# One score loop for both halves of K, a loop for the down projection, and start-up code moved to the end of three engines' programs

## The chip, the cores and the metric

The kernel runs on one core of one Trainium2 chip. A core has engines that each follow a program of their own and meet through semaphores: TensorE (PE in the profile, with PEld for its weight loads), VectorE (DVE), ScalarE (ACT), GpSimd (POOL) and SyncE (SP), which here only issues DMA transfers. Sixteen DMA engines move data between the chip's memory and the core's on-chip memory. The metric is the device time of one execution in microseconds; lower is better. Three runs of the kernel before took 2518.41, 2518.26 and 2518.09 us, so its median is 2518.26 us.

## What is computed

One token passes a block of attention with a long cache and a small feed-forward block, and a gate mixes the two results. All data is bf16.

```python
g = sigmoid((x * gate_w).sum(-1))
q = (x @ wq)                                   # 32 heads of 128
scores = q . k_cache * 128 ** -0.5             # 65536 keys a head
o = softmax(scores) . v_cache                  # 65536 values a head
a = o @ wo                                     # 4096 -> 512
b = (silu(x @ w_gate) * (x @ w_up)) @ w_down   # 512 -> 1792 -> 512
out = g * a + (1 - g) * b
```

The K cache and the V cache are 512 MiB each, and every byte of them is used once, so nearly all of the work is the reading of 1 GiB.

## The kernel before

**Tiling.** The 65536 rows of K of one head are cut into two halves, u = 0 and 1, called A and B. A half is one transfer of 8 MiB into the tile `ring`: each of the 128 partitions takes 256 rows of 128 numbers. V is cut in the same way. The regions of `ring` for the two K halves overlap by half of a region, and those of the two V halves by 48 of 64 KB, so a load may start only when a part of the half before it has been used up.

**Order of the loads.** SP holds one queue. For head r it waits until 24 of the 32 transposes of that head are done and issues the A half of the next head's K (lines 168 and 169), waits for `va1` and issues the B half of V, waits until 8 transposes of the next head are done and issues the B half of its K (lines 177 and 178), then waits for `vbd` and issues the A half of V (lines 179 and 180). Line 145 is the helper that issues. The first head's loads, and those of the weights, are issued in pieces; the last V half is loaded in six pieces (`PARTS`), each with a semaphore of its own, behind 11 of the 14 chunks of `w_down`. The last three chunks of `w_down` come at the very end.

**Scores.** A half of K is 16 chunks of 16 rows. For each chunk DVE transposes 128x1024 words from `ring` to one of four buffers `kt` (helper `turn`, line 314), once PE has freed that buffer (`qkd`). PE then runs four matmuls of 512 columns into the one PSUM bank `psS` (helper `scores`, line 401). Their weights are windows of 128 columns of `zq`, a tile of zeros that has q in four of its columns; where the window lies decides into which row of `psS` the scores of the chunk fall. All addresses are constants: 64 matmuls for the A half and 64 for the B half stand in the program one after another. The first matmul of a head clears the bank, the last one closes it.

**Softmax and values.** After the last chunk of the B half DVE takes the row maximum of `psS` (line 338), POOL the maximum over partitions (line 216), ACT the exponentials (line 251), DVE transposes them to `pb` (line 340). PE multiplies V by them: in `flow` (line 417) four rows of V a matmul into `psW`, and for the last rows of the B half in `values` (line 408) one row a matmul into `psO`. Between the two, DVE copies `psW` (line 327, for the last head line 355) and eight small fp32 matmuls fold it into `psO` (line 452).

**PE's program.** It is a set of blocks joined by branches. After a start-up part (lines 363 to 396: a ramp, x, the gate, q for all heads) the blocks run so for each head: `pe_ka` (scores of the A half), `pe_vb` (B half of V of the head before), `pe_kb` (scores of the B half, then the A half of V). Before the last head's `pe_kb` stands `pe_wo`, where the output projection of 31 heads is done by pairs of matmuls (`both`, line 512 and, through `whole`, line 428), four pairs in an iteration of a loop. After the last head's A half of V stands `pe_mlp`: gate and up projection (line 488), then 11 chunks of the down projection written out one after another (through `whole`, line 428), whose sum ACT copies (line 266) and PE adds into the output banks (lines 423 and 424). Then come `pe_vb` for the last head and `pe_end` with the last three chunks of `w_down`, the last head's part of the output projection and the output itself.

**DVE's and POOL's programs** begin with their start-up parts (lines 281 to 308, lines 201 to 213). DVE then loops over the heads; POOL's reductions for the 32 heads stand one after another.

Of the kernel before, what the change touches and what calls it, by code (L numbers as in the profile page):

```python
# [5 lines left out]
P = 128  # L6
# [7 lines left out]
FETCH = 256  # L14
# [12 lines left out]
def bass_gated_mix__mha_block_cached__swiglu_ffn__decode_kernel(  # L27
# [27 lines left out]
    with ExitStack() as ctx:  # L55
# [6 lines left out]
        def sem(name):  # L62
# [47 lines left out]
                 "ktd qkd va1 vbd s_mx s_ar s_nb s_exp s_pb s_L s_li s_otn s_o s_om s_y s_br s_fl s_flc s_id4 s_qr s_qc s_wod s_o31 s_y0 s_y1 s_fin s_out s_hot")  # L110
# [88 lines left out]
        @block.gpsimd  # L199
        def _(pool):  # L200
            nc.gpsimd.memset(xTz[:], 0.0).then_inc(sm["s_qd"], 1)
            nc.gpsimd.memset(qd[:], 0.0).then_inc(sm["s_qd"], 1)
            for m, n in enumerate(MARKS[1:]):
                nc.gpsimd.memset(hbuf[:, m], 0.0).then_inc(sm[n], 16 * L)
            nc.gpsimd.memset(hot[:], 0.0).then_inc(sm["s_hot"], 1)
            pool.wait_ge(sm["s_id"], 1)
            pool.wait_ge(sm["s_hot"], 1)
            nc.gpsimd.tensor_copy(hot[:, 31:128:32], ident[:, P - 4:P])
            for je in range(4):
                off = 64 * (je // 2) + je % 2  # L210
                last = nc.gpsimd.tensor_copy(sel[:, je, :].rearrange("p (g d) -> p g d", g=4),
                                             ident[:, off:off + 63:2].unsqueeze(1).to_broadcast([P, 4, 32]))
            last.then_inc(sm["s_sel"], 1)
            for h in range(H):
                pool.wait_ge(sm["s_mx"], h + 1)
                nc.gpsimd.partition_all_reduce(amx, mxs, P, RMAX).then_inc(sm["s_ar"], 1)  # L216
                pool.wait_ge(sm["s_exp"], h + 2)
                nc.gpsimd.partition_all_reduce(Lt, rsum, P, RADD).then_inc(sm["s_L"], 1)  # L218
# [54 lines left out]
        def _(dve):  # L273
            chain = [0]

            def link(ins):
# [4 lines left out]
            nc.vector.memset(psW[:], 0.0).then_inc(sm["s_fl"], 1)  # L281
            nc.vector.memset(ones1[:], 1.0).then_inc(sm["s_ones"], 1)
            link(nc.vector.memset(onesr[:], 1.0))
            nc.vector.tensor_tensor_scan(ramp[:], onesr[:], onesr[:], 0.0, ALU.mult, ALU.add).then_inc(sm["s_ramp"], 1)
            link(nc.vector.memset(zq[:], 0.0))
            link(nc.vector.memset(lt[:], 0.0))
            nc.vector.memset(guT[:, 0:1], 0.0).then_inc(sm["s_exp"], 1)
            nc.vector.memset(o31[:], 0.0).then_inc(sm["s_otn"], 1)
            nc.vector.memset(st[:], 1.0).then_inc(sm["s_L"], 1)
            nc.vector.memset(psO[:, 0:1], 0.0).then_inc(sm["vbd"], 1)  # L290
            nc.vector.memset(om[:], 0.0).then_inc(sm["qkd"], NB)
            dve.wait_ge(sm["s_rampT"], 1)
            nc.vector.tensor_tensor(ident[:], ramp[:], psQ[:, 0, 0:1].to_broadcast([P, P]),
                                    ALU.is_equal).then_inc(sm["s_id"], 1)
            dve.wait_ge(sm["s_id"], 1)
            nc.vector.reduce_sum(id4[:], ident[:].rearrange("p (g e) -> p e g", g=4)[:, 0:4, :],
                                 AX_X).then_inc(sm["s_id4"], 1)
            dve.wait_ge(sm["s_x"], 32)
            nc.vector.tensor_tensor_reduce(out=xg[0:1, :], in0=xrow[0:1, :], in1=gwrow[0:1, :],
                                           scale=1.0, scalar=0.0, op0=ALU.mult, op1=ALU.add,  # L300
                                           accum_out=sc[0:1, 0:1]).then_inc(sm["s_z"], 1)
            dve.wait_ge(sm["s_xT"], 1)
            dve.wait_ge(sm["s_qd"], 2)
            nc.vector.tensor_copy(xTb, psM[:, 0:Dc]).then_inc(sm["s_xTb"], 1)
            dve.wait_ge(sm["s_e1"], 1)
            link(nc.vector.tensor_scalar_add(sc[:, 2:3], sc[:, 1:2], 1.0))
            link(nc.vector.reciprocal(sc[:, 3:4], sc[:, 2:3]))
            link(nc.vector.tensor_scalar(sc[:, 4:5], sc[:, 3:4], -1.0, 1.0, ALU.mult, ALU.add))
# [7 lines left out]
            with nc.Fori(0, H, engines=[ET.DVE]) as i:  # L316
# [20 lines left out]
                dve.wait_ge(sm["qkd"], i * PER + (PER + NB))  # L337
                nc.vector.reduce_max(mxs, psS[:], AX_X).then_inc(sm["s_mx"], 1)  # L338
                dve.wait_ge(sm["s_exp"], i + 2)
                nc.vector.transpose(pb[:], pa[:]).then_inc(sm["s_pb"], 1)  # L340

            dve.wait_ge(sm["s_otn"], H + 1)
# [19 lines left out]
        def _(pe):  # L362
# [75 lines left out]
            with nc.body("pe_ka", valid_engines=only):  # L438
# [3 lines left out]
                for n, c in enumerate(A_ORDER):  # L442
                    scores(n, c, i, n == 0, False)
# [120 lines left out]
```

## Time and profile before

| | us |
|---|---|
| median of 3 runs | 2518.26 |
| the profiled execution, its own time | 2518.01 |
| its span, first to last instruction | 2516.6 |
| PE busy | 1511.9 |
| DVE busy | 1249.7 |
| DMA queue of SP, share of 16 engines' span | 99.9% |
| mean rate of the DMA | 432 GB/s |
| granted TensorE clock, mean | 0.781 |

A row of the timeline has a start, a duration, the engine, the line of the kernel, the operation with out<-in, a count, and in brackets the idle time before it with what ended it. A row of a window lists the window, its length, and the busy time and count of each engine; at its end stand the granted TensorE clock (1.00 is full speed), the mean busy share of the 16 DMA engines and the rate. In the list of a line's instructions, PEldq is the sequencer that issues PE's instructions, and the durations are the shortest, the median and the longest.

### The profile page before, as it was taken

The page shows a single profiled execution, that of the slowest core. Times are in us where ns is not written, and L with a number is a line of the kernel's source. Part 1 is how long each engine was busy: PE and PEld are TensorE (multiplying, and loading weights), DVE is VectorE, ACT ScalarE, POOL GpSimd, SP SyncE. Part 2 cuts the span into 40 slices and gives each one's busy share as a digit, 9 for nine tenths or more (in the row PEclk, how much of TensorE's full clock was granted, in tenths as well). Part 3 has the DMA queues.
Part 4 walks back from the last instruction along what each step waited for, and adds up shares of the span by engine and source line. Part 5 has one row for each costly group of instructions (what it writes and reads, how often), then busy time and mean ns, then how long its engine had stood idle before and what let it go on. Part 6 is the DMA issues. An engine that isn't in the chain of part 4 may idle for free.

```text
span 2516.6 us, 25250 instructions
## 1 busy us (share of the span) xinstructions
PE 1511.9 (60%) x10158; PEld 573.9 (23%) x10158; DVE 1249.7 (50%) x1213; ACT 43.0 (2%) x142; POOL 25.9 (1%) x81
## 2 busy tenths in 40 slices
PE   4565655745656556566565575565655655656568
PEld 1222222212222222222222121222212222212222
DVE  5454553644545536445455364464553644545534
ACT  0000000000000000000000000000000000000000
POOL 0000000000000000000000000000000000000000
PEclk8877877878778778778787787877877778778788
DMA  9999999999999999999999999999999999999999
GB/s 419 434 433 433 434 433 434 433 434 434 434 433 434 434 433 435 433 432 433 433 433 433 433 433 433 433 433 433 433 434 433 433 433 434 433 433 433 433 432 394
DMA packets 20748, 1087.73 MB, mean 432 GB/s; under 512 B 2307, under 2 KB 2694, under 8 KB 2950
## 3 DMA queue, kind: packets, MB, share of 16 engines
q1 hardware_dynamic: 20736, 1087.64, 99.9%
q8 instruction: 4, 0.07, 0.0%
q14 instruction: 2, 0.02, 0.0%
q10 hardware_dynamic: 6, 0.00, 0.0%
HBM read 1087.64 MB, written 0.00 MB: 432 GB/s over the span
## 4 chain that ended last, share of the span: by engine, by line
DMA 75%; DVE 15%; issue 7%; PE 2%; DVEq 1%; SPq 0%; ACT 0%; POOL 0%
DMA ring<-in_A_k_cache_dram 74%; DVE kt L314 15%; PE psS L401 2%; DMA ring<-in_A_v_cache_dram 1%; DVEq L311 0%; SPq L145 0%; PE psW L417 0%; DVE st L325 0%; PE psY L423 0%; ACT pa L251 0%; DVE pb L340 0%; DVE st L338 0%; DVEq L324 0%; DVE fin L359 0%; SPq L136 0%
## 5 line engine op out<-in xcount | busy, mean ns | idle before, releaser
L401 PE MATMUL psS<-kt,zq 128*128 128x512 bf16 x4096 | 1132.6, 425 | 854.6 <-DVE kt L314 835.3
L314 DVE STREAM_TRANSPOSE kt<-ring 128x1024 uint32<-128x1024 uint32 x1024 | 1163.1, 1206 | 939.7 <-DMA ring<-in_A_k_cache_dram 939.7
L401 PEld LDWEIGHTS psS<-kt,zq 128*128 128x128 bf16 x4096 | 385.1, 104 | 1588.3 <-DVE kt L314 1129.7
L417 PE MATMUL psW<-ring,pb 128*4 128x512 bf16 x3584 | 256.2, 448 | 102.7 <-DVE pb L340 102.4
L417 PEld LDWEIGHTS psW<-ring,pb 128*4 128x4 bf16 x3584 | 94.8, 98 | 262.6 <-issue 187.8
L327 DVE COPY brow<-psW 128x512 f32<-128x512 f32 x32 | 22.1, 691 | 120.5 <-PE psW L417 120.5
L408 PEld LDWEIGHTS psO<-pb,ring 128*128 128x128 bf16 x2048 | 57.0, 98 | 0.5 <-DMA ring<-in_A_v_cache_dram 0.2
L408 PE MATMUL psO<-pb,ring 128*128 128x1 bf16 x2048 | 56.6, 163 | 0.2
L330 DVE TENSOR_SCALAR lt<-psO,st,sc 128x4 f32 x32 | 9.4, 294 | 89.1 <-PE psO L408 89.1
L452 PE MATMUL psO<-id,brow 128*128 128x1 f32 x256 | 33.8, 253 | 25.5 <-DVE brow L327 24.7
L340 DVE STREAM_TRANSPOSE pb<-pa 128x512 bf16<-128x512 bf16 x32 | 22.8, 711 | 48.7 <-ACT pa L251 48.7
L249 ACT ACTIVATE st<-st 128x1 f32<-128x1 f32 x32 | 6.5, 203 | 2358.5 <-POOL st L216 2358.5
L338 DVE TENSOR_REDUCE st<-psS 128x1 f32<-128x512 f32 x32 | 22.1, 692 | 37.4 <-PE psS L401 37.4
L452 PEld LDWEIGHTS psO<-id,brow 128*128 128x128 f32 x256 | 31.0, 191 | 41.7 <-DVE brow L327 40.4
L216 POOL PARTITION_ALL_REDUCE st<-st x32 | 11.2, 351 | 2420.2 <-DVE st L338 2420.2
L251 ACT ACTIVATE pa<-psS,st 128x512 bf16<-128x512 f32 x32 | 22.0, 687 | 1.0
L428 PE MATMUL psF<-ring,om 128*1 (+1 forms) x32 | 12.7, 396 | 2.9 <-DMA ring<-in_A_wo_dram 2.9
L512 PE MATMUL psY<-ring,hot 128*128 (+1 forms) x32 | 13.1, 411 | 0.0
L218 POOL PARTITION_ALL_REDUCE st<-st x32 | 12.3, 383 | 36.4 <-ACT pa L251 36.4
L256 ACT COPY zq<-qd 128x16 bf16 x31 | 7.7, 248 | 0.0
L251 ACT ACTIVATION_READ_ACCUMULATOR pa<-psS,st 128x1 f32 x32 | 6.2, 193 | 0.0
L428 PE MATMUL psF<-ring,kt 128*1 128x512 bf16 x11 | 4.2, 564 | 3.0 <-DVE kt L353 3.0
(87 smaller groups left out, 52.8 us busy)
## 6 DMA issues: line engine op xcount, KB each, us to landing
ring<-in_A_k_cache_dram SPq DMA_DIRECT2D x4, 4096.0 KB, 27.4
ring<-in_A_v_cache_dram SPq DMA_DIRECT2D x3, 2048.0 KB, 17.6
ring<-in_A_wq_dram SPq DMA_DIRECT2D x1, 4096.0 KB, 12.4
ring<-in_A_wo_dram SPq DMA_DIRECT2D x2, 2048.0 KB, 10.6
ring<-in_B_w_gate_dram SPq DMA_DIRECT2D x1, 1792.0 KB, 21.4
ring<-in_B_w_up_dram SPq DMA_DIRECT2D x1, 1792.0 KB, 25.4
ring<-in_B_w_down_dram SPq DMA_DIRECT2D x1, 1408.0 KB, 13.1
ring<-in_A_v_cache_dram SPq DMA_DIRECT2D x1, 1280.0 KB, 20.4
```

The lines of the kernel that those rows point to most:

```text
L218: nc.gpsimd.partition_all_reduce(Lt, rsum, P, RADD).then_inc(sm["s_L"], 1)
L251: nc.scalar.activation(pa[:], psS[:], ACT.Exp, bias=nbias, scale=SCALE, accum_out=rsum).then_inc(sm["s_exp"], 1)
L314: nc.vector.transpose(o, src).then_inc(sm["ktd"], 1)
L327: nc.vector.tensor_copy(brow[:], psW[:]).then_inc(sm["s_flc"], 1)
L338: nc.vector.reduce_max(mxs, psS[:], AX_X).then_inc(sm["s_mx"], 1)
L340: nc.vector.transpose(pb[:], pa[:]).then_inc(sm["s_pb"], 1)
L401: last = nc.tensor.matmul(psS[:], zw[je][c], ktb[n % NB][:, je // 2, :, je % 2], start=first and je == 0, stop=stop and je == 3)
L408: last = nc.tensor.matmul(psO[:, 0:1], at(base + r * 256, Dh), pb[:, col:col + 1], start=first and n == 0, stop=stop and n == len(rows) - 1)
L417: last = nc.tensor.matmul(psW[g:g + 4, :], pb[:, col:col + 97:32], at(base + r * 256, 4 * Dh), start=first and n < 4, stop=stop and n >= l ...
L428: return nc.tensor.matmul(psF[0:1, :], lhs, rhs, start=first, stop=stop)
L452: nc.tensor.matmul(psO[:, 0:1], brow[:, e * Dh:(e + 1) * Dh], id4[:, e:e + 1], start=e == 0, stop=False)
L512: return nc.tensor.matmul(psY[:], hot[:, bass.ds(31 - j, P)], w, start=first, stop=stop)
```

## The change

Four things are changed.

- **One loop for the scores.** A new block `pe_scores` holds four chunks and is run four times for each half. The register `top` (31 for A, 15 for B) and the loop's counter give the window of `zq`, so each of the 16 weight loads of an iteration has an address from a register. `turns` counts the chunks for the wait on `ktd`. The branch at its end goes on by `top`. Since no matmul of the loop can be the first or the last by a constant, a matmul of a row of zeros by 512 zeros clears `psS` ahead of the A half (`clear`) and another one closes it behind the B half (`seal`), and DVE's maximum waits for that last one (`s_ss`) instead of for the count of chunks. The chunks fall into other rows of `psS`; `place` takes that into account for the columns of `pb`. The row of zeros is a row of `xg` that DVE clears at the start.
- **A loop for the down chunks.** Ten of the 11 matmuls in `pe_mlp` become a loop with one matmul an iteration; the eleventh follows it.
- **The output projection's loop** takes two pairs in an iteration and 15 iterations, instead of four pairs and seven.
- **The order of the programs.** On PE, DVE and POOL the program begins with a branch to the start-up part, which now stands behind the code of the heads; from there a branch leads back to the heads. On PE the start-up part stands just ahead of `pe_mlp`, `pe_wo` and `pe_end`. DVE's loop over the heads is written with a register and a branch. The alignment to 256 bytes on PE goes.

```diff
+        zero = xg[32:33, :].bitcast(BF16)
-        zw = [[zq[:, je, 31 - c:31 - c + P] for c in range(2 * NCH)] for je in range(4)]
...
         @block.gpsimd
...
+            nc.br("pool_begin", engines=only)
+            with nc.body("pool_heads", valid_engines=only):
+                for h in range(H):
...
+                nc.br("pool_end", engines=only)
+            with nc.body("pool_begin", valid_engines=only):
+                nc.gpsimd.memset(xTz[:], 0.0).then_inc(sm["s_qd"], 1)
...
+                nc.br("pool_heads", engines=only)
...
         @block.vector
...
+            nc.br("dve_begin", engines=only)
...
-                dve.wait_ge(sm["qkd"], i * PER + (PER + NB))
+                dve.wait_ge(sm["s_ss"], i + 1)
                 nc.vector.reduce_max(mxs, psS[:], AX_X).then_inc(sm["s_mx"], 1)
...
+                nc.vector.memset(xg[32:33, :], 0.0)
...
         @block.tensor
...
+            nc.regs_mov(turns, 0)
+            nc.br("pe_begin", engines=only)
...
+            def clear(out):
+                return nc.tensor.matmul(out, zero[:, 0:P], zero[:, P:P + 512], start=True, stop=False)
+            def seal(out):
+                return nc.tensor.matmul(out, zero[:, 0:P], zero[:, P:P + 512], start=False, stop=True)
+            def add(out, lhs, rhs):
+                return nc.tensor.matmul(out, lhs, rhs, start=False, stop=False)
+            def place(r, u):
+                return (r % CH) * 32 + NCH * u + (r // CH + (4 if u else 12)) % NCH
...
             with nc.body("pe_ka", valid_engines=only):
                 i = nc.snap(head, min_val=0, max_val=L)
                 pe.wait_ge(sm["s_zq"], i + 1)
                 pe.wait_ge(sm["s_exp"], i + 1)
-                for n, c in enumerate(A_ORDER):
-                    scores(n, c, i, n == 0, False)
+                clear(psS[:])
+                nc.regs_mov(top, 31)
+                nc.br("pe_scores", engines=only)
+
+            with nc.body("pe_scores", valid_engines=only):
+                with nc.Fori(4, 4 + NCH, NB, engines=only) as j:
+                    t = nc.snap(turns, min_val=0, max_val=PER * H - NB)
+                    z = (nc.snap(top, min_val=15, max_val=31) - j % NCH).with_bounds(min_val=NB - 1, max_val=31)
+                    for n in range(NB):
+                        pe.wait_ge(sm["ktd"], t + (n + 1))
+                        for je in range(4):
+                            last = add(psS[:], zq[:, je, bass.ds(z - n, P)], ktb[n][:, je // 2, :, je % 2])
+                        last.then_inc(sm["qkd"], 1)
+                    nc.regs_alu(turns, turns, NB, op=ALU.add)
+                nc.br_lt(top, 31, on_true="pe_va", on_false="pe_kad", engines=only)
...
             with nc.body("pe_kb", valid_engines=only):
+                nc.regs_mov(top, 15)
+                nc.br("pe_scores", engines=only)
+
+            with nc.body("pe_va", valid_engines=only):
+                seal(psS[:]).then_inc(sm["s_ss"], 1)
                 i = nc.snap(head, min_val=0, max_val=L)
-                for n, c in enumerate(B_ORDER):
-                    scores(NCH + n, NCH + c, i, False, n == NCH - 1)
                 pe.wait_ge(sm["s_pb"], i + 1)
...
-                for j in range(WD_CUT):
-                    last = whole(guT[:, 32 * j:32 * j + 1], wd_ap[:, j, :], stop=(j == WD_CUT - 1))
-                last.then_inc(sm["s_y"], 1)
+                with nc.Fori(0, WD_CUT - 1, engines=only) as j:
+                    whole(guT[:, bass.ds(j * 32, 1)], wd_ap[:, bass.ds(j, 1), :].rearrange("p c n -> p (c n)"))
+                j = WD_CUT - 1
+                whole(guT[:, 32 * j:32 * j + 1], wd_ap[:, j, :], stop=True).then_inc(sm["s_y"], 1)
...
                 both(0, first=True)
-                with nc.Fori(1, 29, 4, engines=only) as j:
-                    for n in range(4):
-                        both(j + n)
-                both(29)
-                both(30)
+                with nc.Fori(1, 31, 2, engines=only) as j:
+                    both(j)
+                    both(j + 1)
                 both(31, stop=True).then_inc(sm["s_wod"], 1)
```

More of the change, by code (lines that the diff above doesn't have):

```diff
@@ L200, in _ @@
         def _(pool):
[L201 to L218, printed above, removed]
+            only = [ET.Pool]
@@ L279, in link @@
                 dve.wait_ge(sm["s_dch"], chain[0])
[L281 to L308, printed above, removed]
+            only = [ET.DVE]
+            turn_h = nc.alloc_registers("dve_head", engines=only)
+            nc.regs_mov(turn_h, 0)
+            nc.br("dve_begin", engines=only)
             def turn(byte, c, n, i):
@@ L405, in values @@
-            def values(base, u, rows, first, stop):
-                for n, r in enumerate(rows):
-                    col = (r % CH) * 32 + NCH * u + r // CH
-                    last = nc.tensor.matmul(psO[:, 0:1], at(base + r * 256, Dh), pb[:, col:col + 1],
-                                            start=first and n == 0, stop=stop and n == len(rows) - 1)
-                return last
+            only = [ET.PE]
+            head = nc.alloc_registers("pe_head", engines=only)
+            left = nc.alloc_registers("pe_left", engines=only)
```

167 lines of the change are left out of this document (111 added, 56 removed).

## Prediction

> **What bounds the kernel now.** First the page, for the span and the DMA queues, and the list of DMA issues, whose last column is the median time from issue to landing.
>
> ```profile
> span 2516.6 us, 25250 instructions
> DMA packets 20748, 1087.73 MB, mean 432 GB/s; under 512 B 2307, under 2 KB 2694, under 8 KB 2950
> q1 hardware_dynamic: 20736, 1087.64, 99.9%
> q8 instruction: 4, 0.07, 0.0%
> ring<-in_A_v_cache_dram SPq DMA_DIRECT2D x63, 32.4
> ring<-in_A_k_cache_dram SPq DMA_DIRECT2D x62, 29.3
> ```
>
> SP's queue keeps all 16 DMA engines busy for 99.9% of the span: the kernel runs at the rate of its transfers. The second thing to see is the slack. A half of K or V is 8.39 MB, at 432 GB/s 19.4 us of transfer, but from issue to landing a K half takes 29.3 us and a V half 32.4 us. So a K half stands 9.9 us in the queue behind other transfers, a V half 13.0 us. Whatever makes PE or DVE release a region later by less than that leaves no gap.
>
> Then a head from the middle, in the timeline:
>
> ```profile
> 1194.74 2.77 PE L417 MATMUL psW<-ring,pb 128*4 128x512 bf16 x48
> 1199.22 1.77 PE L408 MATMUL psO<-pb,ring 128*128 128x1 bf16 x64
> 1214.16 18.14 DVE L314 STREAM_TRANSPOSE kt<-ring 128x1024 uint32<-128x1024 uint32 x16 [12.73 <-DMA ring<-in_A_k_cache_dram]
> 1215.47 17.97 PE L401 MATMUL psS<-kt,zq 128*128 128x512 bf16 x64 [14.48 <-DVE kt L314]
> 1223.48 0.33 SPq L145 DMA_DIRECT2D ring<-in_A_k_cache_dram  x1
> 1233.48 0.69 DVE L338 TENSOR_REDUCE st<-psS 128x1 f32<-128x512 f32 x1 [1.17 <-PE psS L401]
> ```
>
> DVE waits 12.73 us for the landing, then sets the pace of the scores: 18.14 us for 16 chunks, 1.13 us each, and PE follows. A K issue (1223.48) comes 9.3 us into the stage, after the eighth transpose.
>
> Last the tail, where no later load hides anything:
>
> ```profile
> 2462.49 18.14 DVE L314 STREAM_TRANSPOSE kt<-ring 128x1024 uint32<-128x1024 uint32 x16 [22.63 <-DMA ring<-in_A_k_cache_dram]
> 2464.41 17.35 PE L401 MATMUL psS<-kt,zq 128*128 128x512 bf16 x64
> 2484.96 6.41 PE L417 MATMUL psW<-ring,pb 128*4 128x512 bf16 x64 [3.20 <-DVE pb L340]
> 2500.82 4.22 PE L428 MATMUL psF<-ring,kt 128*1 128x512 bf16 x11 [2.95 <-DVE kt L353]
> 2506.23 1.90 PE L417 MATMUL psW<-ring,pb 128*4 128x512 bf16 x32
> 2508.44 1.04 PE L417 MATMUL psW<-ring,pb 128*4 128x512 bf16 x16 [0.31 <-DMA ring<-in_A_v_cache_dram]
> 2510.28 1.13 PE L452 MATMUL psO<-id,brow 128*128 128x1 f32 x8 [0.80 <-DVE brow L355]
> 2511.54 2.29 PE L408 MATMUL psO<-pb,ring 128*128 128x1 bf16 x64
> 2514.46 0.08 PEld L423 LDWEIGHTS psY<-ring,kt 128*1 128x1 bf16 x1 [0.23 <-DMA ring<-in_B_w_down_dram]
> ```
>
> From the last landing of K (2462.49) on there runs a chain of compute: transposes, softmax, V, the MLP, the down chunks, the last V rows. It meets the last transfers almost in step: PE waited for a piece of V only 0.31 us at 2508.44, and its 64 value matmuls took 2.29 us with the waits for three landings in them, against 1.77 us without. So the tail has two limits half a microsecond apart, and what the change adds to the chain shows at the end.
>
> **The change, part by part.** All is reckoned against the profiled execution, 2518.01 us (1.4 more than its span); the median, 2518.26, lies 0.25 above it.
>
> Price of a loop on PE: the sequencer's instructions of the loop for `wo`, between 2445.0 and 2447.3, and the pace of that loop's matmuls.
>
> ```profile
> L515 PEldq COMPARE_BRANCH  x2: 218/218/219, 2445.0 to 2446.9; - x2
> L515 PEldq FUSED_REGOPS  x2: 83/83/83, 2445.2 to 2447.2; - x2
> L515 PEldq ALU_OP  x1: 36/36/36, 2446.8 to 2446.8; - x1
> L428 PEldq FUSED_REGOPS  x3: 80/80/80, 2445.6 to 2446.4; - x3
> L512 PEldq MOVE  x4: 29/29/29, 2445.4 to 2446.6; - x4
> L512 PEldq FUSED_REGOPS  x4: 51/51/51, 2445.5 to 2446.7; - x4
> 2446.24 0.38 PE L428 MATMUL psF<-ring,om 128*1 x1
> 2446.87 0.38 PE L428 MATMUL psF<-ring,om 128*1 x1
> ```
>
> Branch to branch is 1.9 us (2445.0 to 2446.9). In it lie 14 such instructions, 0.90 us by their durations (218 + 83 + 36 + 3x80 + 4x29 + 4x51), and the issue of eight matmuls; so each costs 0.07 us beside its duration. PE itself needs 0.63 us a pair (2446.24 to 2446.87), 2.5 us an iteration: the sequencer ran ahead there.
>
> *Score loop.* A chunk needs four addresses (0.051 + 0.07 each), a value to wait for (0.036 + 0.07) and a quarter of the loop's edge (branch 0.29, counter 0.11, chunk count 0.11, window 0.24: 0.19): 0.78 us of issue, below DVE's 1.13. So DVE still sets the pace, at no cost. Bounds: nothing, or 1.2 us a chunk if each address takes a move as well (0.10 more), 0.8 us a stage; that is far under the 9.9, and 0.8 in the tail. For a K load to come too late, the first eight transposes would have to lose 9.9 us, that is, a chunk would have to take 2.4 us.
>
> *`clear` and `seal`.* `clear` runs while PE waits 14.48 us for the first chunk: nothing. `seal` is one more matmul between the last chunk and the maximum; four of them make DVE wait 1.17 us, so 0.29. In every head but the last it lies under the 13.0 us of the next V load; in the tail it counts, 0.3. Bounds 0 and 0.6, if the two branches ahead of it (0.29 each) are not covered by the last chunk's matmuls.
>
> *`wo` loop.* Two pairs an iteration need half of the pairs' issue and a whole edge, 2x0.37 + 0.40 = 1.1 us, against PE's 1.26: nothing. If it did fall behind, K's last scores would start later; PE has 0.2 us a chunk to catch up there (17.35 us from 2464.41 on, though it started 1.9 us after DVE).
>
> *Down loop and clock in the tail.*
>
> ```profile
> 2501.60 0.13 PEld L428 LDWEIGHTS psF<-ring,kt 128*1 128x1 bf16 x1 [0.30 <-issue]
> 2502.02 0.13 PEld L428 LDWEIGHTS psF<-ring,kt 128*1 128x1 bf16 x1 [0.30 <-issue]
> 2500.88:2504.30 3.42, 3.42 (x9) 1.04 (x10) 0.00 (x0) 0.00 (x0) 0.00 (x0) 0.50 1.04 441
> 2504.30:2507.70 3.40, 2.73 (x36) 0.86 (x37) 0.00 (x0) 0.57 (x1) 0.00 (x0) 1.00 0.97 412
> ```
>
> An iteration is FUSED_REGOPS, ALU_OP and the branch: 0.083 + 0.036 + 0.218 + 3x0.07 = 0.55 us for a single matmul. Before, the 11 matmuls took 4.22 us and stood ready when `guT` came. Now a move and an address come first (0.1 + 0.15), then ten iterations, 5.5, then the eleventh, 0.5: 6.2, that is 2.0 us more. Bounds: 0.43 us an iteration, the pace of the matmuls before (2501.60, 2502.02), gives +0.7; 0.7, with a second address instruction, +3.5.
>
> The nine down matmuls ran at clock 0.50 with PE wholly busy, and the clock rose to 1.00 for the V rows. With the loop PE streams 0.43 of each 0.55 us, 78%, so the rise may come late. The 48 matmuls of `flow` cost 2.77 us fast (1194.74) and 4.8 slow (6.41 us for 64 at 2484.96). I take the middle, 3.8.
>
> [...]
>
> *Jumps at the start and DVE's extra memset.*
>
> ```profile
> 0.92 0.48 DVE L281 MEMSET psW<- 128x512 f32 x1 [0.92 <-PEq L549]
> 7.86 0.68 DVE L299 CUSTOM_DVE_ANT_0 xg<-xrow,gwrow 1x512 f32<-1x512 bf16 x1 [4.44 <-DMA gwrow<-in_gate_w_dram]
> 24.13 1.25 DVE L314 STREAM_TRANSPOSE kt<-ring 128x1024 uint32<-128x1024 uint32 x1 [14.17 <-DMA ring<-in_A_k_cache_dram]
> 33.72 0.43 SPq L145 DMA_DIRECT2D ring<-in_A_v_cache_dram  x1
> ```
>
> DVE waits 4.44 us for x and then 14.17 us for K. A jump that has to load code, or the memset (at most the 0.48 us of `psW`'s, 128 rows of the same length), costs nothing below 4.4 us, and below 14 us nothing at the end; then it would move the first issue after a transpose, which like the one at 33.72 must come while the first loads still run. POOL's part only prepares tiles for the first head's q, which waits for the same landing.
>
> *Code loads.*
>
> ```profile
> q8 instruction: 1, 0.02, 1.6%
> 2512.00:2513.00 1.00, 0.95 (x36) 0.87 (x34) 0.00 (x0) 0.00 (x0) 0.00 (x0) 0.50 0.72 249
> 2513.00:2514.00 1.00, 0.94 (x25) 0.69 (x22) 0.13 (x1) 0.00 (x0) 0.00 (x0) 0.50 0.28 98
> ```
>
> The first row is of the 4 us from 20 to 24: a packet of code took 1.6% of 16 engines' 4 us, so 1.0 us of one engine. In the last microsecond only 28% of the engines, four or five, still move data: they look like those that carried the four packets. A shorter program has fewer such packets, but a landing waits for the latest engine; only when none is left in the stream does everything land earlier, by about 1 us. I count nothing; bounds 0 and -1.0.
>
> *Sum.* The chain reaches `flow` 0.3 + 2.0 = 2.3 us later: 2508.5. It no longer waits for V; 3.8 us bring it to 2512.3 (before: 2509.5). Copy and fold, 0.80 + 1.13, values in 1.77: 2516.0, where before they ended at 2513.83. That is 2.2; the waits for the last chunks of `w_down` (0.23 for the last) go, so 2.0. **2518.0 + 2.0 = 2520.0 us**, +0.08%.
>
> **The rivals.**
>
> *The chain gets no longer, or the code leaves the stream.* For it: the two limits lie half a microsecond apart, and with a fast `flow` the sum is only +1.0; -1.0 for the code then ends near 2518. With the lower price of the loop as well 2517. Against it: one late engine is enough to hold every landing.
>
> *The loop starves the queue: slower.* Place: K's issue after the eighth transpose. If a chunk takes over 2.4 us, each microsecond beyond the 9.9 opens a gap twice a head, 64 us in all: at 2.6 us a chunk, 1.9 us too much, 2518 + 64x1.9 = 2640. Against it: 0.78, and 1.2 at the most.
>
> *Code is fetched anew at each long jump: slower.* PE's rounds now jump between `pe_scores` and blocks before and behind it. Three packets a head are 93 in 31 heads, 1.0 us of one engine each, 5.8 us spread over 16; PE's own wait stays under the 9.9. 2520.0 + 5.8 = 2525.8. Against it: a head's matmuls before, a thirty-second of all, run over the same code 32 times, yet the span has four such packets in all. [...]
>
> **How the numbers follow.** Forecast (tail longer by 1 to 4.5 us) 0.60; chain hidden or code gone, 2516.8 to 2519, 0.30; starved 0.03; fetched anew 0.04; something that makes it faster by over 0.2%, 0.02; the rest 0.01. 0.2% is 5.0 us, about what a measurement can tell here from no change: below 2513.2 or above 2523.3. The low end of the range is the rival's 2517, the high end the upper price of the loop, +1.5, and a slow `flow`, +1.0, on 2520.0, with half a microsecond for the seal and the addresses: 2523.0. Same takes 0.90, slower 0.08, faster 0.02: the transfers alone, 1087.64 MB in 99.9% of the span, leave nothing to win that size.
>
> **What would show it.** L314 keeps 18.1 us for 16 chunks, q1 99.9%, K 29 us to landing. The down matmuls stand 0.55 us apart, `flow` of the last head starts near 2508.5 and waits for no landing. PE's code packets are fewer than four. The prediction is wrong if the share of q1 falls, if L314 slows, or if the values at the end still wait for V.

## The result, and the profile after

| | before | after |
|---|---|---|
| median of the runs, us | 2518.28 (2517.84 to 2519.28, 22 runs) | 2521.84 (2520.58 to 2523.20, 22 runs) |
| profiled execution, us | 2518.01 | 2521.66 |
| span, us | 2516.6 | 2520.2 |

The ratio of after to before is 1.0014, with an interval of 1.0008 to 1.002: 3.6 us slower, inside the bound of 0.2% below which the prediction counts two times as the same.

First the DMA view of the changed kernel: queues with packets, MB and share of 16 engines, then issues with the median microseconds to landing.

```profile
q1 hardware_dynamic: 20736, 1087.64, 99.8%
q8 instruction: 2, 0.03, 0.0%
...
ring<-in_A_k_cache_dram SPq DMA_DIRECT2D x62, 29.2
```

The stream is what it was: 99.8% against 99.9%, 29.2 us to landing against 29.3. At most 0.3 us is lost in the 31 heads ahead of the tail (the last landing of K below). Code packets (q8) are two instead of four.

The timeline of the changed kernel, a head from the middle and then the tail (start, duration, engine, line, operation, count, and in brackets the idle time before it with what ended it; line 407 are the scores, 434 the down chunks, 416 `flow`, 465 the fold of `psW` into `psO`, 423 the values):

```profile
1214.54 18.14 DVE L299 STREAM_TRANSPOSE kt<-ring 128x1024 uint32<-128x1024 uint32 x16 [12.66 <-DMA ring<-in_A_k_cache_dram]
1216.05 13.34 PE L407 MATMUL psS<-kt,zq 128*128 128x512 bf16 x48 [14.62 <-DVE kt L299]
1223.85 0.33 SPq L144 DMA_DIRECT2D ring<-in_A_k_cache_dram  x1
...
2462.80 18.14 DVE L299 STREAM_TRANSPOSE kt<-ring 128x1024 uint32<-128x1024 uint32 x16 [22.32 <-DMA ring<-in_A_k_cache_dram]
2482.51 0.69 DVE L324 TENSOR_REDUCE st<-psS 128x1 f32<-128x512 f32 x1 [1.57 <-PE psS L404]
2485.67 5.32 PE L416 MATMUL psW<-ring,pb 128*4 128x512 bf16 x64 [3.20 <-DVE pb L326]
2500.79 6.76 PE L434 MATMUL psF<-ring,kt 128*1 x11 [3.30 <-DVE kt L377]
...
2509.16 4.98 PE L416 MATMUL psW<-ring,pb 128*4 128x512 bf16 x48
...
2514.94 1.05 PE L465 MATMUL psO<-id,brow 128*128 128x1 f32 x8 [0.80 <-DVE brow L379]
2515.86 1.77 PE L423 MATMUL psO<-pb,ring 128*128 128x1 bf16 x64
```

DVE transposes 16 chunks in 18.14 us as before and only the first of them waits; K's issue (1223.85) still comes 9.3 us after the first transpose. In the tail the last K half lands 0.3 us later than before (2462.80 against 2462.49), and the down chunks begin at the same moment (2500.79 against 2500.82). Then the chain falls back: 6.76 us for the 11 down chunks (4.22), and 4.98 us for the 48 matmuls of `flow`, which before took 1.90 for 32 and 1.04 for 16. No row of `flow` or of the values waits for a landing any more. The kernel now ends on its chain of compute.

How slow the clock was there, in windows of 3.41 us of the changed kernel (window, length, busy time and count of PE, PEld, DVE, ACT and POOL, granted clock, share of the DMA engines, GB/s):

```profile
2500.04:2503.45 3.41, 2.44 (x5) 0.40 (x5) 0.36 (x1) 0.00 (x0) 0.00 (x0) 0.50 1.03 437
2503.45:2506.86 3.41, 3.14 (x6) 0.48 (x6) 0.00 (x0) 0.00 (x0) 0.00 (x0) 0.50 0.97 414
2506.86:2510.27 3.41, 2.75 (x18) 0.48 (x20) 0.00 (x0) 0.57 (x1) 0.00 (x0) 0.50 0.96 402
2510.27:2513.68 3.41, 3.41 (x36) 1.13 (x32) 0.00 (x0) 0.00 (x0) 0.00 (x0) 0.50 0.75 273
2513.68:2517.09 3.41, 2.61 (x66) 2.15 (x59) 0.69 (x1) 0.00 (x0) 0.00 (x0) 1.00 0.02 6
```

Four such windows, all at 0.50, and full clock only when `flow` is almost done. Only the second lies wholly under the loop: in the first PE waits until 2500.79, the third holds the pause for ACT's copy, and the fourth is `flow` alone, after which the clock rises. The busy column must not be read as streaming here: 3.14 of 3.41 us in the second window is the sum of six modelled durations of 0.58 us or so, while a matmul at half clock keeps PE for 0.43 us (their distance in the tail before) and the next one comes after 0.64. So PE streams 67% of the loop.

### The profile page after: what moved, and what is told of

Read it like the earlier page. It is cut to its first block, busy times and chain, and to the rows that moved or that the text cites. A ratio compares the mean times of both kernels' runs of the same rounds, so it can differ in the third digit from the quotient of the medians.

```text
span 2520.2 us, 30251 instructions
## 1 busy us (share of the span) xinstructions
PE 1533.4 (61%) x10222; PEld 621.1 (25%) x10222; DVE 1251.9 (50%) x1214; ACT 43.0 (2%) x142; POOL 26.4 (1%) x81
## 3 DMA queue, kind: packets, MB, share of 16 engines
q1 hardware_dynamic: 20736, 1087.64, 99.8%
## 4 chain that ended last, share of the span: by engine, by line
DMA 73%; DVE 14%; issue 7%; PE 5%; DVEq 0%; SPq 0%; ACT 0%; POOL 0%
DMA ring<-in_A_k_cache_dram 72%; DVE kt L299 14%; PE psS L407 3%; PE psF L434 1%; DVEq L296 0%; PE psY L569 0%; DMA ring<-in_A_wo_dram 0%; PE psW L416 0%; SPq L144 0%; PE psY L544 0%; DVE st L311 0%; DVE kt L372 0%; PE psY L429 0%; PE psO L423 0%; PE psO L465 0%
## 5 line engine op out<-in xcount | busy, mean ns | idle before, releaser
L299 DVE STREAM_TRANSPOSE kt<-ring 128x1024 uint32<-128x1024 uint32 x1024 | 1164.8, 1207 | 922.8 <-DMA ring<-in_A_k_cache_dram 922.7
L407 PEld LDWEIGHTS psS<-kt,zq 128*128 x4096 | 425.5, 104 | 1510.6 <-issue 1227.0
L416 PE MATMUL psW<-ring,pb 128*4 128x512 bf16 x3584 | 264.2, 459 | 102.3 <-DVE pb L326 102.3
L465 PE MATMUL psO<-id,brow 128*128 128x1 f32 x256 | 33.7, 253 | 25.6 <-DVE brow L313 24.8
L401 PE MATMUL psS<-xg 1*128 1x512 bf16 x32 | 12.5, 391 | 2.2 <-ACT zq L239 2.2
L404 PE MATMUL psS<-xg 1*128 1x512 bf16 x32 | 12.3, 385 | 0.0
L434 PE MATMUL psF<-ring,kt 128*1 (+1 forms) x11 | 6.3, 590 | 3.8 <-DVE kt L377 3.3
```

Source lines behind the costliest of these rows:

```text
L299: nc.vector.transpose(o, src).then_inc(sm["ktd"], 1)
L401: return nc.tensor.matmul(out, zero[:, 0:P], zero[:, P:P + 512], start=True, stop=False)
L407: return nc.tensor.matmul(out, lhs, rhs, start=False, stop=False)
L416: last = nc.tensor.matmul(psW[g:g + 4, :], pb[:, place(r, u):place(r, u) + 97:32], at(base + r * 256, 4 * Dh), start=first and n < 4, stop ...
L434: return nc.tensor.matmul(psF[0:1, :], lhs, rhs, start=first, stop=stop)
L465: nc.tensor.matmul(psO[:, 0:1], brow[:, e * Dh:(e + 1) * Dh], id4[:, e:e + 1], start=e == 0, stop=False)
```

## The experiments

The first four kernels take the change apart. They ran beside the kernel before (2518.31 us, 2517.95 to 2519.06, 33 runs).

**The down chunks written out again, the rest of the change kept.**

```diff
-                with nc.Fori(0, WD_CUT - 1, engines=only) as j:
-                    whole(guT[:, bass.ds(j * 32, 1)], wd_ap[:, bass.ds(j, 1), :].rearrange("p c n -> p (c n)"))
-                j = WD_CUT - 1
-                whole(guT[:, 32 * j:32 * j + 1], wd_ap[:, j, :], stop=True).then_inc(sm["s_y"], 1)
+                for j in range(WD_CUT):
+                    last = whole(guT[:, 32 * j:32 * j + 1], wd_ap[:, j, :], stop=(j == WD_CUT - 1))
+                last.then_inc(sm["s_y"], 1)
```

> The changed kernel with its ten-iteration down loop written out again as 11 matmuls, all else as changed. Theory (the whole loss is the down loop, by its issue and by the clock it leaves low): the chain of the tail is only 0.4 us (the closing matmul) plus 0.3 us (later landing) longer than before, most of it under the half microsecond between the two limits: 2518.3 to 2519.0. Rival (the score loop, the closing matmul or the jumps carry part of it): 2519.5 or more.

Measured: 2518.30 us (11 runs), ratio to the kernel before 1.0, interval 0.9991 to 1.0009. Its timeline:

```profile
2500.25 4.22 PE L434 MATMUL psF<-ring,kt 128*1 128x512 bf16 x11 [2.94 <-DVE kt L377]
...
2505.66 1.90 PE L416 MATMUL psW<-ring,pb 128*4 128x512 bf16 x32
2508.66 1.04 PE L416 MATMUL psW<-ring,pb 128*4 128x512 bf16 x16 [1.10 <-DMA ring<-in_A_v_cache_dram]
...
2511.93 2.18 PE L423 MATMUL psO<-pb,ring 128*128 128x1 bf16 x64
```

With the 11 chunks back to back the clock is up for `flow`, and PE again waits for V, now 1.10 us. The score loop, `clear` and `seal`, the loop for `wo` and the new order of the programs together cost nothing that can be measured.

**The down loop alone, in the kernel before.** The diff is the one above, read the other way, and nothing else.

> The kernel before with the down loop alone. Theory: 0.64 us an iteration makes the down stage 2.3 us longer, the clock stays at 0.50 for the 48 matmuls of flow, another 2.0; less the 0.7 us that the chain had free: about +3.3, 2521.3 to 2521.8. Rival: 2520.5 or less.

Measured: 2521.51 us (2520.81 to 2522.66), ratio 1.0013, interval 1.0004 to 1.0022. Its timeline has the same two rows; the first two of the eleven down matmuls stand ahead of them, at 2500.56 and 2501.20.

```profile
2501.82 5.45 PE L428 MATMUL psF<-ring,kt 128*1 x9 [0.25 <-issue]
...
2508.88 4.34 PE L417 MATMUL psW<-ring,pb 128*4 128x512 bf16 x48
```

The whole loss is here, 3.2 of the 3.6 us; the rest is within the intervals.

**The changed kernel with two chunks in an iteration of the down loop.**

```diff
-                with nc.Fori(0, WD_CUT - 1, engines=only) as j:
-                    whole(guT[:, bass.ds(j * 32, 1)], wd_ap[:, bass.ds(j, 1), :].rearrange("p c n -> p (c n)"))
+                with nc.Fori(0, WD_CUT - 1, 2, engines=only) as j:
+                    for k in range(2):
+                        whole(guT[:, bass.ds((j + k) * 32, 1)],
+                              wd_ap[:, bass.ds(j + k, 1), :].rearrange("p c n -> p (c n)"))
```

> The changed kernel with two down chunks in an iteration, five iterations. Theory with the clock: a pair takes 0.85 us to issue (0.64 and one more address and matmul, 0.21), which is just what two matmuls take at clock 0.50, so PE is busy throughout, the clock rises and flow runs fast again: flow in 2.8 us, total 2518.8 to 2519.5. Rival (the clock plays no part, only the issue does): half of the loss stays, 2520.

Measured: 2518.15 us (2517.95 to 2518.60), ratio 1.0, interval 0.9991 to 1.0009. Its timeline:

```profile
2500.60 3.46 PE L434 MATMUL psF<-ring,kt 128*1 x8 [3.29 <-DVE kt L377]
2504.22 0.93 PE L434 MATMUL psF<-ring,kt 128*1 x3 [0.16 <-issue]
...
2506.34 1.90 PE L416 MATMUL psW<-ring,pb 128*4 128x512 bf16 x32
```

That is 0.65 us under the least that was expected. Eight chunks in 3.46 us are 0.43 each: with two matmuls to one loop's edge PE stays fed, here at half clock. A loop as such costs nothing; one with a single matmul in it does.

**The first of these kernels with PE's start-up part at the head of its program** (no branch to the last blocks; DVE and POOL stay as changed).

```diff
-            nc.br("pe_begin", engines=only)
...
+            pe.wait_ge(sm["s_ones"], 1)
+            pe.wait_ge(sm["s_ramp"], 1)
...
+            nc.br("pe_ka", engines=only)
...
-            with nc.body("pe_begin", valid_engines=only):
```

> The first of these kernels (down chunks written out) with PE's start-up part back at the head of its program, so that PE does not begin with a jump. Theory (the jump is hidden): 6.6 us of PE's waiting at the start goes, PE's packets of code move from the first 12 us to between 20 and 100 us, and the time is that of the first within 0.4 us. Rival (the early jump costs or wins): a difference of 0.5 us or more.

Measured: 2518.25 us (2517.96 to 2518.72), ratio 1.0, interval 0.999 to 1.0009, against 2518.30 with the branch. PE's order makes no difference. In its profiled execution `flow` fell on the half clock by chance:

```profile
2506.89 4.09 PE L414 MATMUL psW<-ring,pb 128*4 128x512 bf16 x48
...
2512.70 1.83 PE L421 MATMUL psO<-pb,ring 128*128 128x1 bf16 x64
```

The span was still 2517.1 us, against 2516.8 with `flow` at full clock (the first of these kernels): written-out chunks start it early enough.

**Is it the loop's issue or the clock?** The changed kernel, its down loop untouched, with one matmul more in each iteration.

```diff
                     whole(guT[:, bass.ds(j * 32, 1)], wd_ap[:, bass.ds(j, 1), :].rearrange("p c n -> p (c n)"))
+                    nc.tensor.matmul(psM[0:1, 0:256], om[:, 0:1], wd_ap[:, 0, 0:256], start=True, stop=True)
```

> The changed kernel with one matmul more in each iteration of the down loop (256 columns, into a bank that nothing reads any more), so that PE streams nearly the whole iteration; it is work that the reference doesn't have, and its result isn't used. Theory (the loop's gaps keep the clock at half, and that makes the last flow slow): the iterations stay at 0.63 us or a little more, but the clock rises to 1.00 within some 4 us, the 48 matmuls of flow take about 2.8 instead of 4.98 us, and the time falls by about 2 us, to 2519.5 to 2520. Rival (the slow flow has another cause than the loop's gaps): flow stays near 5 us, and the time at 2521.8 or a little more.

Measured: 2518.41 us (2517.95 to 2520.09, 11 runs; before 2518.27), ratio 1.0002, interval 0.9993 to 1.0011. More work made the kernel 3.4 us faster, where 2 had been expected. Its timeline, then its windows:

```profile
2506.73 0.38 PE L434 MATMUL psF<-ring,kt 128*1 128x512 bf16 x1
...
2508.29 2.77 PE L416 MATMUL psW<-ring,pb 128*4 128x512 bf16 x48
...
2512.77 1.74 PE L423 MATMUL psO<-pb,ring 128*128 128x1 bf16 x64
```

```profile
2500.00:2503.40 3.40, 2.44 (x9) 0.46 (x10) 0.28 (x1) 0.00 (x0) 0.00 (x0) 0.80 1.00 424
2503.40:2506.80 3.40, 3.22 (x13) 0.59 (x11) 0.00 (x0) 0.00 (x0) 0.00 (x0) 0.70 1.00 423
2506.80:2510.20 3.40, 2.74 (x42) 0.98 (x44) 0.00 (x0) 0.57 (x1) 0.00 (x0) 1.00 0.97 407
```

The loop is as slow as in the changed kernel: its last matmul is done at 2507.11, 2.64 us later than with written-out chunks (2500.25 + 4.22). But the clock comes back inside the loop, `flow` takes 2.77 us, and the values end at 2514.51, 0.4 us after those of the written-out kernel, where `flow` had waited 1.10 us for V. So the 2.6 us of issue alone are nearly covered by the last transfers. So is a slow `flow` alone: with 4.09 us in the kernel with PE's start-up part at the head the span was 2517.1 us. Late and slow together, in the kernel with the down loop alone (4.34 us), it was 2519.3. The transfers cover either of the two, not their sum, and it is the loop's gaps that kept the clock from coming up ahead of `flow`.

**How much room the score loop has.** Two kernels were meant to lengthen its issue, by 8 and 14 register additions a chunk, on top of the first experiment's kernel.

```diff
                         last.then_inc(sm["qkd"], 1)
+                        for _ in range(14):
+                            nc.regs_alu(spare, spare, 1, op=ALU.add)
```

> The kernel with the down chunks written out, and eight register additions more in front of each chunk of the score loop; their value is not used. By my price of an addition, 0.036 + 0.07 us, a chunk takes 0.78 + 8 x 0.11 = 1.6 us of issue instead of 0.78, more than DVE's 1.13, so PE now paces the scores. Theory (the queue stands 9.9 us ahead of a K half): a stage of 16 chunks grows by 16 x 0.5 = 8 us; the first eight chunks, on which an issue waits, by 4 us, hidden; q1 stays at 99.8% or more, and only the last stage's 8 us come out, some of them under the half microsecond of room at the end: 2525 to 2527 us. Rival (the loop's issue already counts at 0.78): every stage shows, and 64 stages of even 2 us lost would give 2640.

> The same with fourteen additions a chunk: 0.78 + 14 x 0.11 = 2.3 us of issue a chunk. By the deciding point in the prediction (2.4 us a chunk, where the first eight transposes lose 9.9 us) the queue is still never empty, and only the tail grows, by 16 x 1.2 = 19 us: about 2537. Second theory: what decides is not one stage but the round of a head. PE has two stages of scores and, between them, the softmax and two runs of V, about 16 us, in the 77.4 us that a head's transfers take; with 2.3 us a chunk that is 2 x 37 + 16 = 90 us, 12 us too much, 31 times: about 2900, with q1 near 87%. At 2.1 us a chunk it would be 2 x 34 + 16 = 84, and 2720. The limit by that theory is 1.9 us a chunk.

Measured: 2518.31 and 2518.10 us, one execution each. These say nothing about issue. In the trace of the second, between 1214 and 1234 us, the sequencer's only plain additions are the values to wait for:

```profile
L451 PEldq ALU_OP  x12: 32/32/36, 1216.2 to 1231.9; - x12
```

The 224 additions of a stage are not there; nothing reads their value, and they did not reach the chip. What the runs are worth is that they repeat the first experiment. In the first of them `flow` was slow again, 4.12 us for the 48 matmuls from 2506.64 on, at no cost in time; in the second it was fast.

**The same question with PE's own work:** 4 and 7 matmuls of zeros more in each chunk.

```diff
                         for je in range(4):
+                        for _ in range(7):
+                            add(psS[:], zero[:, 0:P], zero[:, P:P + 512])
+                        for je in range(4):
```

> The kernel with the down chunks written out, and four matmuls of zeros more in each chunk of the score loop (one row by 512 columns, added to the same bank; it changes nothing in the scores, but is work that the reference doesn't have). A matmul takes 0.21 us at full clock, so a chunk takes PE 8 x 0.213 = 1.7 us instead of DVE's 1.13, a stage 9 us more. The queue's slack is 9.9 us for a K half, whose issue waits for eight chunks (4.6 us later), and 13.0 us for a V half, whose issue waits for all sixteen (9.1 us later). Both theories below expect it hidden in every head but the last, with q1 at 99.8% or more; the last stage's 9 us come out, some of them under the half microsecond of room: 2526 to 2527 us. If the score loop had no room at all, 64 stages of 9 us would give 3100.

> The same with seven matmuls of zeros a chunk: 11 x 0.213 = 2.35 us a chunk, a stage of 16 chunks 19.5 us longer than with DVE's 1.13. By the deciding point of the prediction, 2.4 us a chunk (K's issue waits for eight chunks, which lose 9.8 of 9.9 us), the queue is still never empty and only the last stage shows: about 2537 us. Second theory: V decides, since its issue waits for the whole stage, 19.5 us later against 13.0 us of slack; the limit is 1.13 + 13.0 / 16 = 1.9 us a chunk, and 2.35 loses 6.5 us in each of some 62 stages: about 2920 to 2940 us, q1 near 86%. By a head's round it is the same order: two stages of 37.6 us and about 16 us of V and softmax are 91 us against the 77.4 us of the transfers.

Measured: 4073.03 and 5523.42 us, one execution each, where 2526 and at most 2940 had been expected. The page of the kernel with four, a piece of its timeline, and two windows on either side of it:

```profile
PE 3868.0 (95%) x14317; PEld 1018.0 (25%) x14318; DVE 1335.0 (33%) x1214; ACT 43.1 (1%) x142; POOL 26.4 (1%) x81
...
q1 hardware_dynamic: 20736, 1087.64, 62.9%
```

```profile
1544.04 1.03 PE L407 MATMUL psS<-xg 1*128 1x512 bf16 x4
...
1545.00 1.83 PE L407 MATMUL psS<-kt,zq 128*128 128x512 bf16 x4
1546.76 1.88 PE L407 MATMUL psS<-xg 1*128 1x512 bf16 x4
```

```profile
1530.00:1540.00 10.00, 10.00 (x45) 3.10 (x41) 4.98 (x4) 0.00 (x0) 0.00 (x0) 1.00 1.03 419
1550.00:1560.00 10.00, 10.00 (x24) 2.35 (x23) 3.74 (x3) 0.00 (x0) 0.00 (x0) 0.50 0.98 426
```

The matmuls were priced at full clock. PE was busy for 95% of the span, but the clock, which had come up under `flow`, fell some 15 us into the stage, to 0.45 us a matmul, although PE never paused: a chunk took 3.6 us, not 1.7, and PE became the bound (4071.6 / 32 = 127 us a head against 77). Both theories lie below that, so the runs don't tell them apart; they had to be asked on another engine.

**The same question on DVE,** where the work added is not PE's: a sum over 4, 7 and 3 times 128 numbers ahead of each transpose.

```diff
+        pad = sb("pad", [P, NB, 4], F32)
...
+                nc.vector.reduce_sum(pad[:, n % NB, :], ident[:].unsqueeze(1).to_broadcast([P, 4, P]), AX_X)
                 nc.vector.transpose(o, src).then_inc(sm["ktd"], 1)
```

> The kernel with the down chunks written out, and on DVE a sum over 4 x 128 numbers ahead of each transpose, whose result isn't used: it is work that the reference doesn't have. By the maximum over 512 numbers (0.69 us) less the overlap of neighbours, a chunk takes about 1.13 + 0.57 = 1.7 us, a stage 9.1 us more, without more work for PE. K's issue waits for eight chunks, 4.6 us later against 9.9 us of slack; V's waits for all sixteen, 9.1 us later against 11.6 us (A half: issue at 1164.16, next landing of K at 1175.75 in the trace of the kernel with the down chunks written out) and 13.1 us (B half: 1123.93 and 1137.02). Both theories: no gap, q1 at 99.8%, and only the last stage's 9 us come out, less half a microsecond: about 2527 us.

> The same with 7 x 128 numbers: about 1.13 + 0.97 = 2.1 us a chunk, a stage 15.5 us longer. First theory, the deciding point of the prediction (2.4 us a chunk, by K's issue after eight chunks: 7.8 us against 9.9): no gap, only the tail is longer, about 2533 us. Second theory, V decides (its issue waits for the whole stage: 15.5 us later, against 11.6 and 13.1 us of slack): 3.9 + 2.4 = 6.3 us lost in each of 31 heads, about 195 us, and the tail: about 2730 us, q1 near 92%. The limit by the second theory is 1.13 + 11.6 / 16 = 1.85 us a chunk.

> As the two runs before on DVE, with a sum over 3 x 128 numbers ahead of each transpose (not work of the reference, its result isn't used). Four and seven times 128 made a chunk 0.586 and 0.986 us longer, so three give 0.453: 1.59 us a chunk, and from K's landing to V's issue about 7.7 us more. Theory from those two runs: V's issue (B half, after the sixteenth chunk of K's B half) stood 11.6 us ahead of K's landing, and an issue needs 3.1 us of head start, since 9.9 - 11.6 + 3.1 gives the 1.33 us and 16.8 - 11.6 + 3.1 the 8.3 us that each head lost. Then 7.7 - 11.6 + 3.1 is below zero: no head loses anything, the last landing of K is within 1 us of 2462.7, q1 is at 99.6% or more, and only the last stage shows: 2525 to 2526.5 us. Rival (the loss is in proportion to the longer chunk, or DVE's extra work slows the transfers themselves): about 0.453 / 0.586 of the loss of the run with four, 1.0 us a head, 31 us in all and 7 in the tail: about 2557 us.

One execution each. The last K landing is the start of the last stage, 2462.72 in the written-out kernel; what it moves, over 31, is the loss of a head.

| sum over | a chunk longer by, us | time, us | q1 | last K landing | lost a head, us |
|---|---|---|---|---|---|
| 3 x 128 | 0.45 | 2544.23 | 99.4% | 2483.08 | 0.66 |
| 4 x 128 | 0.59 | 2569.20 | 98.9% | 2503.94 | 1.33 |
| 7 x 128 | 0.99 | 2790.58 | 91.7% | 2720.53 | 8.32 |

From the timelines of the kernels with 4, 7 and 3, in this order, one V issue of SP and the landing of K next to it (the wait in brackets):

```profile
1270.52 0.33 SPq L145 DMA_DIRECT2D ring<-in_A_v_cache_dram  x1
1272.85 0.69 DVE L300 TENSOR_REDUCE pad<-ident 128x4 f32<-128x512 bf16 x1 [7.21 <-DMA ring<-in_A_k_cache_dram]
```

```profile
1295.98 1.09 DVE L300 TENSOR_REDUCE pad<-ident 128x7 f32<-128x896 bf16 x1 [3.80 <-DMA ring<-in_A_k_cache_dram]
1297.61 0.33 SPq L145 DMA_DIRECT2D ring<-in_A_v_cache_dram  x1
```

```profile
1259.65 0.33 SPq L145 DMA_DIRECT2D ring<-in_A_v_cache_dram  x1
1262.95 0.55 DVE L300 TENSOR_REDUCE pad<-ident 128x3 f32<-128x384 bf16 x1 [8.81 <-DMA ring<-in_A_k_cache_dram]
```

The deciding point of the prediction, 2.4 us a chunk, is refuted: at 1.13 + 0.99 = 2.12 the queue runs dry in every head. The second theory is right in which issue comes late first: V's, behind a whole stage of scores (it is the issue of V's B half, after the B half of K; the expectations call it the A half's). In the written-out kernel it stands 11.6 us ahead of K's landing; with 4 x 128 2.3 us are left in the head shown (1.0 to 2.2 in the others), and with 7 x 128 it comes 1.6 us after the landing (up to 3.8 elsewhere). With 7 x 128 both halves lose, as expected there: from the A half's landing of K to the B half's it is 44.3 us on average, from B to A 41.1, against 38.7 in the written-out kernel; with 4 x 128 it is 39.8 and 38.8. Nor is the slack usable to the end: 3.3 us ahead of the landing (3.0 to 4.3 over the heads) already costs 0.66 us a head. The third run fell between its two theories: a fixed head start of 3.1 us fits the runs with 4 and 7, where V's issue comes 9.9 and 16.8 us later behind its landing of K (9.9 - 11.6 + 3.1 = 1.4; 16.8 - 11.6 + 3.1 = 8.3), but by it the run with 3 would have lost nothing. The fit with 7 was luck, since it charges to one issue what two halves lost. So the loss begins softly, somewhere below 1.59 us a chunk; where, and how much of it is the queue empty and how much the transfers themselves being slower beside DVE's extra work, stays open.

## Why the prediction was right, and where it was not

The forecast was no difference by the 0.2% bound, 2520.0 us, in a range up to 2523.0; the kernel takes 2521.84. The 1.8 us between lie in the tail, by these steps:

- *The stream sets the time, and nothing but the tail shows.* Right: q1 99.8%, L299 18.14 us for 16 chunks, K 29.2 us to landing.
- *Score loop 0, `wo` loop 0, jumps 0.* Right: without the down loop the changed kernel takes 2518.30 us, and 2518.25 without PE's jump as well.
- *`seal` +0.3.* The term was 0.40: DVE waits 1.57 us for it instead of 1.17. It didn't reach the end: `flow` of the A half, at a clock that fell otherwise, took 5.32 us instead of 6.41, and the down chunks began when they had before. That was luck of the clock.
- *Down loop, 0.55 us an iteration, +2.0.* Mis-sized, 0.64 and +2.5 (6.76 against 4.22). The sequencer's instructions of the loop's edge, and of the matmul's line, in the changed kernel:

```profile
L549 PEldq FUSED_REGOPS  x10: 78/78/94, 2500.5 to 2506.3; - x10
L549 PEldq ALU_OP  x10: 36/36/36, 2500.8 to 2506.6; - x10
L549 PEldq COMPARE_BRANCH  x10: 76/208/209, 2500.9 to 2506.7; - x10
```

```profile
L434 PEldq FUSED_REGOPS  x10: 46/46/51, 2500.7 to 2506.4; - x10
```

The weights and the moving data each take an address of their own. The prediction had that as its bound (0.7 us, "with a second address instruction") and took the one without; (2506.3 - 2500.5) / 9 = 0.64 is what it costs.

- *`flow` at the middle, 3.8 us.* It took 4.98, the slow price and a little more, and the four small matmuls and the copy ahead of it 1.61 us instead of 1.19. The prediction had the mechanism (78% streaming, "the rise may come late") but took the middle of the two prices. With written-out chunks both were measured: of the five traces of kernels that have them and no other work, two had `flow` slow (4.09 and 4.12 us for the 48 matmuls). With the loop only the slow one was: with a second address the share is 67%, and no window under the loop brought the clock up, in this run or in that of the loop alone (4.34), while a filled loop did. The loop's 2.5, these 0.4 and `flow`'s 2.0 (4.98 against 1.90 + 1.04), less the wait of 0.31, are the 4.7 us by which `flow` ends later (2514.14 against 2509.48); the fold and the values, which wait for no landing now, give 0.9 back.
- *"Two limits half a microsecond apart."* Too little, and by rows that stand in the prediction: beside the 0.31 us ahead of `flow`, the values took 2.29 us with waits in them against 1.77 without, and the last chunks of `w_down` waited 0.23. The filled loop shows the room: 2.6 us of delay ahead of a fast `flow` made 0.1 us of time, where the prediction had +1.0 for 2.3 us.
- *Code loads, 0, with a bound of -1.0 "when none is left in the stream".* The two packets all come in the first 12 us, and nothing is left behind them; yet in the changed kernel's window from 2513 a few DMA engines still move data (a share of 0.16; before 0.28), and the written-out kernel is no faster than the one before. What makes a few engines late at the end was not the code packets, or not they alone; it stays open.

```profile
2513.00:2514.00 1.00, 1.00 (x16) 0.24 (x8) 0.00 (x0) 0.00 (x0) 0.00 (x0) 0.65 0.16 56
```

- *Code fetched anew at each long jump* had 0.04, and is refuted for this kernel: PE jumps between its blocks in each of 32 heads, and the changed kernel's trace has two packets in all, both in its first 12 us, where this rival counted on 93.
- *The starved queue* had the right sign, and its price was right in kind, but its place and deciding point were wrong: not K's issue after eight chunks at 2.4 us, but V's B half after sixteen, at less than 1.59. The change, at 1.13, is still below it.

## What to carry to other kernels

When a loop on PE holds one small matmul, count every address register it needs, and ask not only what the issue costs but whether the gaps keep the clock from rising for what comes next; two matmuls in an iteration removed both here. Slack at a queue is to be read at every issue; here the one behind the longest stage ran out first, and losses began with some 3 us of it left. The chain here, which ends level with the last transfers, had room that changed from run to run with the clock (with the down chunks written out, `flow` took 1.90 + 1.04 us in one and 4.09 in another, in spans of 2516.8 and 2517.1 us), so a few microseconds there are priced with both clocks, not with their middle, and two delays that cost nothing alone are priced together.

## What the runs showed of the hardware

- A PE loop that streams 0.43 of every 0.64 us (67%) didn't bring the clock up: the window that lies wholly under it stood at 0.50, and so did the next, in the changed kernel (2503.45 to 2506.86) and in that with the loop alone (2501.89 to 2505.30); filled up, the loop brought it to 1.00 (0.70 in the mean from 2503.40 to 2506.80, 1.00 from there to 2510.20). In the tail the granted clock changed at 2490.64, 2500.88, 2504.30 and 2511.12 in the kernel before and at 2486.38, 2489.80, 2500.04, 2513.69 and 2517.10 in the changed one: 3, 1 and 2 times, and 1, 3, 4 and 1 times 3.41 us apart. The two kernels with register additions, whose down chunks stream without a gap once begun, had different shares. Here are, for the first and then for the second, the window from the fall of the clock on and the one after it:

```profile
2499.18:2502.59 3.41, 2.41 (x6) 0.71 (x7) 0.91 (x2) 0.00 (x0) 0.00 (x0) 0.50 0.97 413
2502.59:2506.00 3.41, 2.75 (x8) 0.59 (x8) 0.00 (x0) 0.57 (x1) 0.00 (x0) 0.50 1.01 432
```

```profile
2499.49:2502.90 3.41, 2.73 (x7) 0.84 (x8) 0.62 (x1) 0.00 (x0) 0.00 (x0) 0.50 1.00 428
2502.90:2506.31 3.41, 2.75 (x30) 0.84 (x32) 0.00 (x0) 0.57 (x1) 0.00 (x0) 1.00 0.98 419
```

  With PE streaming 2.41 of 3.41 us (71%) the clock stayed at 0.50, with 2.73 (80%) it rose to 1.00 in the next window, and `flow` was slow in the first of these traces and fast in the second. What share is enough was not shown.
- A PE that is busy without a pause can stay at half clock: in the kernel with four zero matmuls a chunk the first two stages, from 25.6 to 141.9 us, ran at 0.45 us a matmul from end to end, the clock came up only under `flow`, and it fell again some 15 us into the next stage. (The record of the granted clock reads 1.00 there up to its first change at 166 us; the pace is what tells: 45 matmuls in the 20 us from 40 on, and 46 in those from 220 on, where the record reads 0.50.) PE was wholly busy at such a fall: 10.00 of 10.00 us from 1530, from 1540 and from 1550, at a granted clock of 1.00, 0.75 and 0.50. Half of these matmuls have a single row of zeros as weights; whether that has to do with it, no run separates.
- PE's branch to the last blocks of its program took 6.6 us at the start, under the wait for the first K, where it cost nothing:

```profile
L395 PEldq COMPARE_BRANCH  x1: 6637/6637/6637, 1.1 to 1.1; - x1
```
